# A new written order of the whole program, and engines chosen anew for its movable operations

## The chip, the cores and the metric

The kernel runs on one core of one Trainium2 chip. The metric is the device time of one execution in microseconds (us). The engines are named as in the profile: PE is TensorE (matmuls), PEld its weight loads, DVE is VectorE, ACT is ScalarE, POOL is GpSimd, SP is SyncE, whose queue issues the DMAs here.

## What is computed

Attention in both directions between 512 tokens x and 32 state tokens, for 8 batches and 8 heads of 64, and then a two-layer network with a squared ReLU on the 8 x 544 = 4352 rows that come out (512 wide, 2048 hidden). The weights w_in and w_out come as 64-bit floats.

```python
scores = scale * np.matmul(x, state.transpose(0, 1, 3, 2))
a = softmax(scores);  xread = np.matmul(a, state)
scores2 = scale * np.matmul(state, x.transpose(0, 1, 3, 2))
a2 = softmax(scores2);  sread = np.matmul(a2, x)
x = concatenate([xread, sread], axis=2) -> [4352, 512]
h = np.maximum(x @ w_in, 0.0)
out = h * h @ w_out
```

## The kernel before

Every matmul of the network keeps float32 accuracy with three passes: each operand is split into a high part (`*_hi`, rounded to fp32r by ACT) and a low part (`*_lo`, the rest, by a subtraction on DVE or POOL), and hi x hi, hi x lo and lo x hi are summed in PSUM. The rows xread are never formed: state @ w_in is made once for each batch (`direct_w2`, `second_w2`, later from a DRAM copy; tiles `w2ps`, `w2_<batch>_<hb>`), and the softmax, transposed (`k_hi`, `k_lo`), is multiplied with it.

The names that the change and the prediction touch:

- `warm.i` (line 855) is one dummy matmul of the identity into a tile `pw`. `prep.b.g` (631) transposes x through PE (`px`) and copies it out (`xT`); `states.0` does the same for the states (`pd`, `sD`), and `states.2` transposes those of the other batches on DVE (`sT<-std2`). `scores.b` writes `st`, `keep_s` copies it to `e2`, and `transposed_scores` transposes that to `pst`.
- `softmax.b.g` (717): a reduce to the maximum `m1` and a subtraction into `sp` on DVE, the exponential on ACT, a reduce, a small addition and a reciprocal on DVE, and a multiplication of `sp` (key `sm_mul`, POOL or DVE). Then PE transposes `sp` to `pa`, ACT rounds it to `k_hi`, and DVE subtracts to `k_lo`.
- `decode` (545) turns a 64-bit weight (`wi_raw`, `wo_raw`) into 32 bits (`wf`, `dec`): a clamp (keys `decode_wi`, `decode_wo`; DVE, or POOL where the key is listed), a Prelu on ACT, a shift on DVE, and an "or" with the low word on DVE (SCALAR_TENSOR_TENSOR). `prep_wo.fc` (1031) decodes w_out and splits it into `wo<fc>`: ACT makes the high part, and the key `w_out_lo` says whether POOL or DVE makes the low one.
- `hidden.blk.fc` (1039) makes one tile of 128 hidden units for 512 tokens in PSUM: six matmuls `ph<blk>_<fc>` from `k_hi`, `k_lo` and `w2`, then ReLU and square (ACT, or ACT and DVE), `g_hi` on ACT, and `g_lo = ph - g_hi` on DVE. The pool of `ph` has two buffers, so the tile after next can only begin when `g_lo` has been made. `accumulate.blk.fc` (1095) multiplies `g_hi`, `g_lo` with `wo<fc>` into four PSUM tiles `acc`. After every fourth hidden tile `acc` is copied to `first` or added to a partial sum.
- Batches 5 to 7 run later in a form with seven products in place of eight (`m`, `a_g`, `b_g`, `s`), and the 256 rows of sread come as a block 8.

Nothing is scheduled at run time or by a planner: `PLAN` (lines 25 to 340) is a list of 2835 step names written out. Each entry runs that step on to its next `yield`, and since `LOOSE_FROM` is "never", each engine's program is in exactly the order in which the entries are worked off. All instructions are issued through one helper, so the profile has them all at line 417, and tiles tell them apart. `SECOND` (368 to 404) lists the keys whose operation goes to the second of its two possible engines:

```python
def pick(key, *engs):
    return engs[chosen(key)]          # chosen: key in SECOND

def evac(key, out, src):
    if chosen(key): nc.vector.tensor_copy(out, src)
    else:           nc.scalar.copy(out, src)

for k in plan:
    if k not in begun:
        f, args, after = steps[k]
        begun[k] = f(*args)
    ...
        next(begun[k], None)
```

Of the kernel before, what the change touches and what calls it, by code (L numbers as in the profile page):

```python
# [30 lines left out]
        decode_wi.1 prep.1.0 transposed_scores.0.0 decode_wi.1 load_wo.1 direct_w2.0 softmax.0.1 direct_w2.0
        warm.12 softmax.0.1 direct_w2.0 softmax.0.1 warm.13 softmax.0.0 direct_w2.0 direct_w2.0 warm.14 softmax.0.0
        warm.15 direct_w2.0 softmax.0.0 warm.16 softmax.0.1 direct_w2.0 softmax.0.1 decode_wi.2 warm.17 second_w2.0
        softmax.0.0 softmax.0.0 prep_wo.1 prep_wo.0 prep_wo.0 warm.18 warm.19 second_w2.0 warm.20 second_w2.0
        warm.21 load_raw.3 prep.1.1 second_w2.0 second_w2.0 decode_wi.2 second_w2.0 prep.1.1 softmax.0.1 prep.1.1
        decode_wi.2 softmax.0.1 prep.1.0 load_wo.2 softmax.0.1 prep_wo.2 load_wo.8 decode_wi.2 prep.1.1 load_raw.4
        softmax.0.0 prep_wo.0 prep.1.0 load_wo.3 softmax.0.0 decode_wi.2 prep_wo.1 prep_wo.0 softmax.0.0 scores.1
        keep_s.1.0 decode_wi.3 load_states.2 keep_s.1.1 hidden.0.0 decode_wi.3 hidden.0.0 prep_wo.1 prep_wo.1
        hidden.0.0 decode_wi.3 prep_wo.0 hidden.0.0 transposed_scores.1.1 transposed_scores.1.0 decode_wi.4
        hidden.0.1 softmax.1.1 prep_wo.2 softmax.1.0 load_states.2 hidden.0.1 load_wo.4 softmax.1.1 prep_wo.3  # L40
        prep_wo.1 softmax.1.0 decode_wi.3 prep_wo.1 hidden.0.0 hidden.0.0 softmax.1.0 hidden.0.1 hidden.0.1
        accumulate.0.0 decode_wi.3 direct_w2.1 prep_wo.2 direct_w2.1 load_raw.5 accumulate.0.0 prep_wo.2
        direct_w2.1 direct_w2.1 direct_w2.1 decode_wi.4 direct_w2.1 direct_w2.1 softmax.1.1 hidden.0.1 load_wo.5
        second_w2.1 hidden.0.2 prep_wo.2 softmax.1.0 decode_wi.4 load_wo.7 hidden.0.1 accumulate.0.1 hidden.0.2
        hidden.0.2 decode_wi.4 softmax.1.0 load_raw.6 second_w2.1 second_w2.1 prep_wo.3 hidden.0.2 softmax.1.1
        hidden.0.3 softmax.1.0 accumulate.0.1 second_w2.1 decode_wi.4 prep_wo.2 hidden.0.3 softmax.1.0 exp_s.0.1
        hidden.0.2 hidden.0.2 softmax.1.1 second_w2.1 second_w2.1 load_wo.6 accumulate.0.2 hidden.0.3 exp_s.0.1
        prep_wo.3 softmax.1.1 decode_wi.5 decode_wi.5 prep_wo.3 softmax.1.1 softmax.1.0 hidden.0.3 load_states.2
        prep_wo.3 decode_wi.5 softmax.1.1 decode_wi.5 hidden.0.3 hidden.0.3 load_wo.11 decode_wi.5 prep_wo.4
        accumulate.0.2 hidden.1.0 decode_wi.6 prep_wo.3 direct_w2.2 load_raw.7 prep_wo.4 hidden.1.0 hidden.1.0  # L50
# [5 lines left out]
        decode_wi.7 accumulate.1.0 hidden.1.2 prep_wo.6 transposes.0 hidden.1.2 prep_wo.6 decode_wi.10 second_w2.2
        second_w2.2 prep_wo.6 hidden.1.2 prep_wo.5 second_w2.2 second_w2.2 second_w2.2 transposes.0 hidden.1.3
        hidden.1.2 hidden.1.2 decode_wi.10 hidden.1.3 accumulate.1.1 load_raw.8 prep_wo.4 decode_wi.10 direct_w2.3
        hidden.1.3 prep_wo.5 decode_wi.10 prep_wo.5 direct_w2.3 hidden.1.3 hidden.0.4 transposes.0 direct_w2.3
        direct_w2.3 accumulate.1.1 accumulate.1.2 load_wo.12 direct_w2.3 direct_w2.3 direct_w2.3 second_w2.3  # L60
        hidden.1.3 hidden.1.3 decode_wi.8 load_raw.11 hidden.0.4 transposes.0 second_w2.3 second_w2.3 hidden.0.4
        prep_wo.6 accumulate.1.2 decode_wi.8 second_w2.3 decode_wi.8 decode_wi.10 decode_wi.8 hidden.0.4 load_wo.13
        hidden.0.7 accumulate.1.3 prep_wo.5 prep_wo.6 prep_wo.4 hidden.0.7 accumulate.1.3 hidden.0.4 hidden.0.4
        prep_wo.9 hidden.0.7 decode_wi.11 hidden.0.7 load_raw.9 transposes.0 prep_wo.5 accumulate.1.3 decode_wi.11
        hidden.0.7 hidden.0.7 prep_wo.9 accumulate.1.3 accumulate.1.3 prep_wo.11 decode_wi.11 accumulate.1.3
# [1517 lines left out]
```

## Time and profile before

| | |
|---|---|
| median of 3 runs | 646.66 us (646.49 to 646.94) |
| the profiled execution | 646.96 us |
| its span in the trace | 645.1 us |
| PE busy | 631.9 us, 98% |
| PEld busy | 528.1 us, 82% |
| DVE busy | 465.8 us, 72% (927 instructions) |
| ACT busy | 394.7 us, 61% |
| POOL busy | 184.5 us, 29% (172 instructions) |

The span runs from the first to the last instruction on the engines; 1.9 us of the execution lie around it. A share of busy time is an average over stages that differ: in the first 80 us the weights are decoded and the softmaxes made while PE already multiplies; the middle part is multiplication with work for later batches beside it. In a timeline or a group, a row names the instruction as output<-inputs with buffer numbers left out, its shape, and in brackets the idle time of its engine just before it and what ended that. A stretch's row gives, behind its length, the busy time of PE, PEld, DVE, ACT and POOL, then TensorE's granted clock, the DMA engines' busy share and the GB/s.

### The profile page before, as it was taken

The page shows a single profiled execution, that of the slowest core. Times are in us where ns is not written, and L with a number is a line of the kernel's source. Part 1 is how long each engine was busy: PE and PEld are TensorE (multiplying, and loading weights), DVE is VectorE, ACT ScalarE, POOL GpSimd, SP SyncE. Part 2 cuts the span into 40 slices and gives each one's busy share as a digit, 9 for nine tenths or more (in the row PEclk, how much of TensorE's full clock was granted, in tenths as well). Part 3 has the DMA queues.
Part 4 walks back from the last instruction along what each step waited for, and adds up shares of the span by engine and source line. Part 5 has one row for each costly group of instructions (what it writes and reads, how often), then busy time and mean ns, then how long its engine had stood idle before and what let it go on. Part 6 is the DMA issues. An engine that isn't in the chain of part 4 may idle for free.

```text
span 645.1 us, 12288 instructions
## 1 busy us (share of the span) xinstructions
PE 631.9 (98%) x4453; PEld 528.1 (82%) x4453; DVE 465.8 (72%) x927; ACT 394.7 (61%) x815; POOL 184.5 (29%) x172
## 2 busy tenths in 40 slices
...
DVE  3999888675675688686958543579999866577637
...
GB/s 280 279 285 277 252 276 214 295 274 236 256 181 313 237 205 265 192 233 237 257 256 206 228 105 35 133 65 49 34 49 113 118 115 66 66 50 148 65 1 67
DMA packets 153132, 113.07 MB, mean 175 GB/s; under 512 B 93168, under 2 KB 126448, under 8 KB 153072
## 3 DMA queue, kind: packets, MB, share of 16 engines
...
q10 hardware_dynamic: 288, 0.26, 0.1%
...
## 4 chain that ended last, share of the span: by engine, by line
PE 94%; DVE 2%; issue 1%; DMA 1%; ACT 1%; SPq 0%; POOLq 0%; POOL 0%; DVEq 0%; ACTq 0%
PE acc L417 37%; PE ph L417 30%; PE m L417 18%; PE w2ps L417 3%; PE w4ps L417 2%; PE pr L417 1%; PE st L417 1%; PE pw L417 1%; DMA xn<-in_x_dram 1%; PE px L417 1%; DVE g_lo L417 1%; DVE ph L417 0%; PE pst L417 0%; ACT r L417 0%; PE pa L417 0%
## 5 line engine op out<-in xcount | busy, mean ns | idle before, releaser
L417 PE MATMUL acc<-wo,g_hi 128*128 128x512 f32 x704 | 203.8, 393 | 0.0
L417 PE MATMUL ph<-k_hi,w 128*128 128x512 f32 x512 | 176.1, 392 | 0.4 <-DVE g_lo L417 0.3
L417 PEld LDWEIGHTS acc<-wo,g_hi 128*128 128x128 f32 x704 | 130.6, 188 | 32.6 <-issue 2.5
L417 ACT ACTIVATE r<-ph 128x512 f32<-128x512 f32 (+1 forms) x124 | 70.4, 569 | 97.8 <-PE ph L417 92.6
L417 PE MATMUL acc<-wo,g_lo 128*128 128x512 f32 x352 | 122.1, 391 | 0.0
L417 PEld LDWEIGHTS ph<-k_hi,w 128*128 128x128 f32 x512 | 96.2, 188 | 21.4 <-issue 1.2
L417 PE MATMUL ph<-k_lo,w 128*128 128x512 f32 x256 | 100.3, 392 | 0.0
L417 PEld LDWEIGHTS acc<-wo,g_lo 128*128 128x128 f32 x352 | 65.7, 188 | 14.7 <-DVE dec L417 0.4
L417 DVE TENSOR_TENSOR g_lo<-ph,g_hi 128x512 fp32r<-128x512 f32 (+1 forms) x95 | 60.4, 640 | 23.3 <-ACT g_hi L417 18.9
L417 DVE SCALAR_TENSOR_TENSOR ph<-ph,r 128x512 f32<-128x512 f32 (+1 forms) x48 | 31.1, 648 | 42.3 <-ACT r L417 42.1
L417 PEld LDWEIGHTS ph<-k_lo,w 128*128 128x128 f32 x256 | 48.2, 188 | 8.2
L417 POOL TENSOR_TENSOR w<-w_f,w 128x512 fp32r<-128x512 f32 x21 | 28.9, 1383 | 74.1 <-ACT w L417 37.9
L417 POOL TENSOR_TENSOR sp<-sp,m 128x512 f32<-128x512 f32 x25 | 26.6, 1067 | 72.3 <-DVE m L417 67.5
L417 ACT ACTIVATE g_hi<-r 128x512 fp32r<-128x512 f32 (+1 forms) x76 | 44.0, 582 | 4.9 <-PE acc L417 3.8
L417 POOL TENSOR_TENSOR wf<-wf,wf_hi 128x512 fp32r<-128x512 f32 x8 | 10.9, 1367 | 67.9 <-ACT wf_hi L417 67.9
L417 ACT ACTIVATE ph<-ph 128x512 f32<-128x512 f32 x40 | 23.5, 587 | 10.1 <-PE ph L417 8.6
L417 ACT CAST w<-w_f 128x512 fp32r<-128x512 f32 x40 | 24.2, 614 | 6.6 <-DMA w_f<-w_d 6.5
L417 POOL TENSOR_SCALAR dec<-wo_raw 128x512 f32<-128x512 f32 x10 | 20.5, 2051 | 13.3 <-DMA wo_raw<-in_moe_w_out_dram 13.1
L417 ACT ACTIVATE g<-r 128x512 f32<-128x512 f32 x35 | 21.8, 630 | 0.4
L417 DVE TENSOR_REDUCE m<-sp 128x16 f32<-128x512 f32 x28 | 18.7, 670 | 3.3 <-ACT sp L417 3.1
L417 POOL TENSOR_TENSOR s<-sf,s 128x512 fp32r<-128x512 f32 x6 | 7.8, 1292 | 43.3 <-ACT s L417 43.3
L417 ACT COPY w4o<-w4ps 128x512 f32<-128x512 f32 x16 | 9.1, 588 | 13.8 <-PE w4ps L417 9.7
...
## 6 DMA issues: line engine op xcount, KB each, us to landing
...
```

Source lines behind the costliest of these rows:

```text
L417: op = call(*args, **kw)
```

## The change

`PLAN` is written anew from its 22nd entry on, to the end of the program: the same 2835 entries in another order. `SECOND` is chosen anew. PE, ACT and SP have as many instructions as before; DVE gets six more and POOL six fewer in sum, by many exchanges in both directions. The core of the diff (the table's other rows tell a reader nothing):

```diff
 PLAN = """
     ident warm.0 start.0 start.0 load.0.1 prep.0.0 warm.1 prep.0.0 warm.2 load_raw.0 load.0.1 load_states.0
-        prep.0.1 load_states.0 load_states.0 prep.0.1 warm.3 decode_wi.0 neg_ident load_raw.1 warm.4 prep.0.0
-        warm.5 start.1 warm.6 decode_wi.0 warm.7 prep.0.1 start.1 prep.0.0 load_wo.0 load.1.1 decode_wi.0
...
 SECOND = """
-    decode_wi: 4 10 11 12 13
-    decode_wo: 0 1 2 3 4 5 6 9 11 12
+    decode_wi: 4 11 12 14 15
+    decode_wo: 0 1 2 4 5 8 11 15
...
-    keep_s: 0.1
+    keep_s: 0.1 1.1
...
-    sm_mul: 3.0
+    sm_mul: 0.0 0.1 1.0 2.0 2.1 3.0 4.0 5.0 6.0 7.0 7.1
...
-    w_out_lo: 6 7 10 12 13 14 15
+    w_out_lo: 1 4 5 9 10 11 12 13
...
-    xT: 0.0.0 0.0.1 1.1.0
+    xT: 0.0.0 0.0.1 0.1.1
```

PE at the start of the program, before (px: transposes of x; pw: dummy matmuls; pd: transposes of the states; st: scores):

```order
L417 MATMUL px0_0_1_171<-ident_73,xn0_0_131 128x128 x4
L417 MATMUL pw5_176<-ident_73 128x128
L417 MATMUL pw6_182<-ident_73 128x128
L417 MATMUL pw7_185<-ident_73 128x128
L417 MATMUL px0_1_1_187<-ident_73,xn0_1_134 128x128 x4
L417 MATMUL pd_200<-ident_73,std0_150 128x128 x4
L417 MATMUL pw8_205<-ident_73 128x128
L417 MATMUL pw9_207<-ident_73 128x128
L417 MATMUL st0_1_215<-xT0_1_152,sD_122 32x256
```

and with the change:

```order
L420 MATMUL px0_0_1_176<-ident_73,xn0_0_131 128x128 x4
L420 MATMUL px0_1_1_181<-ident_73,xn0_1_134 128x128 x4
L420 MATMUL pd_190<-ident_73,std0_150 128x128 x4
L420 MATMUL pw6_203<-ident_73 128x128
L420 MATMUL pw21_205<-ident_73 128x128
L420 MATMUL st0_1_214<-xT0_1_152,sD_122 32x256
```

The transposes of x and of the states follow each other, and the first scores come after two dummy matmuls instead of five.

DVE in the first softmaxes, before (m10, sp0: softmax of batch 0; wf, dec: decodes of weights):

```order
L417 TENSOR_SCALAR wf1_315<-wi_raw2_211 128x512
L417 TENSOR_REDUCE m10_0_297<-sp0_0_296 128x16
L417 TENSOR_SCALAR m10_0_297<-m10_0_297 128x16
L417 RECIPROCAL m10_0_297<-m10_0_297 128x16
L417 TENSOR_SCALAR dec0_254<-dec0_254 128x512
L417 COPY xT1_1_341<-px1_1_0_342 128x512
L417 TENSOR_SCALAR wf1_315<-wf1_315 128x512
L417 TENSOR_TENSOR k_lo0_130<-pa0_1_352,k_hi0_129 128x512
L417 SCALAR_TENSOR_TENSOR wf1_315<-wi_raw2_211,wf1_315 128x512
L417 SCALAR_TENSOR_TENSOR dec0_254<-wo_raw0_194,dec0_254 128x512
L417 TENSOR_TENSOR k_lo0_130<-pa0_0_380,k_hi0_129 128x512
```

and with the change:

```order
L420 RECIPROCAL m10_1_289<-m10_1_289 128x16
L420 TENSOR_TENSOR sp0_1_288<-sp0_1_288,m10_1_289 128x512
L420 TENSOR_SCALAR wf1_333<-wi_raw2_201 128x512
L420 TENSOR_SCALAR dec0_258<-dec0_258 128x512
L420 TENSOR_REDUCE m10_0_293<-sp0_0_292 128x16
L420 TENSOR_SCALAR m10_0_293<-m10_0_293 128x16
L420 RECIPROCAL m10_0_293<-m10_0_293 128x16
L420 TENSOR_TENSOR sp0_0_292<-sp0_0_292,m10_0_293 128x512
L420 TENSOR_SCALAR wf1_333<-wf1_333 128x512
L420 SCALAR_TENSOR_TENSOR wf1_333<-wi_raw2_201,wf1_333 128x512
L420 TENSOR_TENSOR k_lo0_130<-pa0_1_352,k_hi0_129 128x512
L420 TENSOR_TENSOR k_lo0_130<-pa0_0_377,k_hi0_129 128x512
```

Both multiplications of sp0 now stand on DVE. The copy of xT1_1 and the or of dec0 no longer stand ahead of the last k_lo0.

DVE ahead of the hidden tiles 4 to 7 of block 0, before (g_lo0_7 is the row that the tile ph0_5 waits for):

```order
L417 TENSOR_SCALAR wf4_860<-wi_raw8_801 128x512
L417 TENSOR_TENSOR w2_1_3_857<-w2ps3_0_0_806,w2_1_3_857 128x256
L417 TENSOR_SCALAR wf4_860<-wf4_860 128x512
L417 SCALAR_TENSOR_TENSOR wf4_860<-wi_raw8_801,wf4_860 128x512
L417 TENSOR_TENSOR wo6_870<-dec6_716,wo6_870 128x512
L417 TENSOR_TENSOR g_lo0_4_865<-ph0_4_831,g_hi0_4_864 128x512
L417 SCALAR_TENSOR_TENSOR ph0_7_884<-ph0_7_884,r0_7_905 128x512
L417 TENSOR_TENSOR g_lo0_7_904<-ph0_7_884,g_hi0_7_903 128x512
```

and with the change:

```order
L420 TENSOR_TENSOR w2_0_3_847<-w2ps3_0_1_830,w2_0_3_847 128x256
L420 TENSOR_TENSOR w2_1_3_864<-w2ps3_0_0_829,w2_1_3_864 128x256
L420 STREAM_TRANSPOSE sT_121<-std2_531 128x768
L420 TENSOR_SCALAR wf4_861<-wf4_861 128x512
L420 SCALAR_TENSOR_TENSOR wf4_861<-wi_raw8_810,wf4_861 128x512
L420 TENSOR_TENSOR wo5_871<-dec5_655,wo5_871 128x512
L420 SCALAR_TENSOR_TENSOR ph0_7_882<-ph0_7_882,r0_7_891 128x512
L420 TENSOR_TENSOR g_lo0_4_849<-ph0_4_822,g_hi0_4_848 128x512
L420 TENSOR_TENSOR w2_1_3_864<-w2ps3_0_1_830,w2_1_3_864 128x256
L420 TENSOR_SCALAR wf5_787<-wf5_787 128x512
L420 SCALAR_TENSOR_TENSOR wf5_787<-wi_raw11_814,wf5_787 128x512
L420 TENSOR_TENSOR g_lo0_7_890<-ph0_7_882,g_hi0_7_889 128x512
```

Between w2_0_3 and g_lo0_7 there are now the transpose sT, wo5 in the place of wo6, one w2 more, and the second half of wf5.

## Rows read from the trace of the kernel before

**Rows 1.** Page: DVE in 40 slices (tenths); chain that ended last, by engine.

```profile
DVE  3999888675675688686958543579999866577637
...
PE 94%; DVE 2%; issue 1%; DMA 1%; ACT 1%; SPq 0%; POOLq 0%; POOL 0%; DVEq 0%; ACTq 0%
```

**Rows 2.** Waits of PE, whole span: released by, us in total, times, longest.

```profile
PE ph L417 <- DVE g_lo L417: 1.2, 3, 0.6
PE w4ps L417 <- DVE g_lo L417: 1.0, 1, 1.0
PE w2ps L417 <- DVE wf L417: 0.6, 1, 0.6
```

**Rows 3.** Stretches of the span: length, then busy us (instructions) of each engine.

```profile
16.10:32.30 16.20, 15.38 (x154) 11.13 (x160) 15.67 (x29) 13.84 (x30) 11.05 (x7) 1.00 0.88 278
32.30:48.40 16.10, 16.06 (x128) 11.96 (x109) 15.64 (x32) 14.08 (x31) 11.15 (x9) 1.00 0.88 285
```

**Rows 4.** Timeline of PE, 0 to 17 us: start, duration, engine, operation, tiles.

```profile
9.49 1.49 PE L417 MATMUL pw<-ident 128*128 128x128 f32 x6
10.77 1.06 PE L417 MATMUL px<-ident,xn 128*128 128x128 f32 x4
...
13.23 1.09 PE L417 MATMUL st<-xT,sD 64*32 64x256 f32 x32
```

**Rows 5.** Timeline of DVE, 14 to 26 us.

```profile
15.02 0.42 DVE L417 TENSOR_SCALAR wf<-wf 128x512 uint32<-128x512 uint32 x1
15.47 0.69 DVE L417 SCALAR_TENSOR_TENSOR wf<-wi_raw,wf 128x512 uint32<-128x512 uint32 x1
16.08 0.68 DVE L417 TENSOR_REDUCE m<-pst 128x16 f32<-128x512 f32 x1
...
24.62 0.68 DVE L417 TENSOR_TENSOR k_lo<-pa,k_hi 128x512 fp32r<-128x512 f32 x1
```

**Rows 6.** Groups on DVE, 24.6 to 67 us: count, busy us, mean ns, idle before.

```profile
L417 DVE SCALAR_TENSOR_TENSOR dec<-wo_raw,dec 128x512 uint32<-128x512 uint32 x7 | 6.8, 975 | 0.1
L417 DVE SCALAR_TENSOR_TENSOR wf<-wi_raw,wf 128x512 uint32<-128x512 uint32 x7 | 6.1, 871 | 0.1
L417 DVE TENSOR_TENSOR w<-w2ps,w 128x256 fp32r<-128x256 f32 x11 | 4.3, 409 | 0.0
L417 DVE TENSOR_SCALAR wf<-wf 128x512 uint32<-128x512 uint32 x7 | 3.8, 546 | 1.3 <-ACT wf L417 1.3
L417 DVE TENSOR_SCALAR wf<-wi_raw 128x512 f32<-128x512 f32 x5 | 3.0, 603 | 0.0
L417 DVE TENSOR_SCALAR dec<-dec 128x512 uint32<-128x512 uint32 x6 | 3.0, 499 | 0.0
```

**Rows 7.** Groups on POOL, 24.6 to 67 us.

```profile
L417 POOL TENSOR_SCALAR dec<-wo_raw 128x512 f32<-128x512 f32 x8 | 16.5, 2071 | 0.5 <-DMA wo_raw<-in_moe_w_out_dram 0.4
L417 POOL TENSOR_TENSOR wo<-dec,wo 128x512 fp32r<-128x512 f32 x6 | 8.9, 1490 | 3.9 <-ACT wo L417 3.9
L417 POOL TENSOR_SCALAR wf<-wi_raw 128x512 f32<-128x512 f32 x3 | 5.8, 1947 | 5.3 <-DMA wi_raw<-in_moe_w_in_dram 5.3
L417 POOL TENSOR_TENSOR sp<-sp,m 128x512 f32<-128x512 f32 x2 | 2.1, 1051 | 2.9 <-DVE m L417 2.9
```

**Rows 8.** Waits of DVE, 24.6 to 67 us.

```profile
DVE wf L417 <- ACT wf L417: 1.3, 2, 1.0
```

**Rows 9.** Timeline of DVE, 66 to 92 us.

```profile
66.92 0.69 DVE L417 TENSOR_TENSOR g_lo<-ph,g_hi 128x512 fp32r<-128x512 f32 x1
...
91.32 0.96 DVE L417 STREAM_TRANSPOSE sT<-std 128x768 f32<-128x768 f32 x1
```

**Rows 10.** Timeline of PE: at 68 us, and at 195.8 us.

```profile
67.98 0.39 PE L417 MATMUL ph<-k_hi,w 128*128 128x512 f32 x1
68.21 0.39 PE L417 MATMUL ph<-k_lo,w 128*128 128x512 f32 x1
...
195.77 0.38 PE L417 MATMUL w4ps<-wf_hi,s 64*128 64x256 f32 x1 [1.05 <-DVE g_lo L417]
```

More of the change, by code (lines that the diff above doesn't have):

```diff
@@ L31 @@
[L31 to L50, printed above, removed]
@@ L56 @@
[L56 to L65, printed above, removed]
@@ new lines @@
+        load_w2.2.1 accumulate.1.11 load_w2.2.0 later_w2.3 later_w2.3 later_w2.3 later_w2.3 later_w2.3 later_w2.3
+        start.3 start.3 prep.2.1 later_w2.3 load_w2.2.0 hidden.1.14 hidden.1.14 hidden.1.14 hidden.1.14
+        scores.2+read.1 transposed_scores.2.0 load_w2.2.2 load_w2.3.0 split_wf.4 load_wf.1.5 softmax.2.0
+        softmax.2.0 softmax.2.0 hidden.1.14 hidden.1.14 transposed_scores.2.1 softmax.2.1 softmax.2.1 softmax.2.0
+        softmax.2.1 load_w2.2.1 softmax.2.0 softmax.2.0 exp_s.2.1 softmax.2.0 softmax.2.0 accumulate.1.12
@@ new lines @@
+        hidden.2.7 hidden.2.7 hidden.2.7 hidden.2.7 later_w2.7 later_w2.7 read.2 sread.2 load.4.1 load.4.1 sread.2
+        sread.2 sread.2 load_w2.2.6 hidden.2.8 hidden.2.8 hidden.2.8 hidden.2.8 accumulate.2.7 load_w2.2.5
+        load_w2.2.5 hidden.2.8 hidden.2.8 w2.1+scores.3 transposed_scores.3.0 last_w2.1 last_w2.1 load_wf.2.0
+        load_wf.2.2 exp_s.3.0 last_w2.1 accumulate.2.8 last_w2.1 load_w2.2.7 last_w2.1 last_w2.1 start.5
+        softmax.3.0 transposed_scores.3.1 softmax.3.1 start.5 start.5 prep.4.0 softmax.3.1 exp_s.3.0 exp_s.3.1
@@ new lines @@
+        start.5 load.5.1 load_w2.2.6 load_w2.2.6 hidden.2.11 hidden.2.11 hidden.2.11 hidden.2.11 hidden.2.11
+        hidden.2.11 hidden.2.10 hidden.2.10 accumulate.2.9 exp_s.3.0 hidden.2.10 hidden.2.10 hidden.2.10
+        hidden.2.10 hidden.2.12 exp_s.3.1 load_w2.2.7 hidden.2.12 accumulate.2.10 exp_s.3.1 transposes.3 load.5.1
+        load.5.1 load.5.1 prep.4.1 load_w2.3.0 transposes.3 hidden.2.12 hidden.2.12 hidden.2.12 hidden.2.12
+        softmax.3.0 softmax.3.0 softmax.3.0 softmax.3.0 softmax.3.1 w2.0+scores.4 last_w2.0 softmax.3.0 softmax.3.0
@@ new lines @@
+        hidden.3.1 load_w2.3.3 load_w2.3.2 start.6 load_w2.3.3 hidden.3.3 hidden.3.3 hidden.3.3 hidden.3.2
+        accumulate.2.15 accumulate.2.15 hidden.3.2 hidden.3.3 hidden.3.3 load_w2.3.4 softmax.4.0 softmax.4.0
+        load_w2.3.5 load.6.1 load_w2.3.6 accumulate.3.0 accumulate.3.1 softmax.4.0 read.3 hidden.3.2 hidden.3.2
+        transposes.4 softmax.4.0 transposes.4 hidden.3.2 hidden.3.2 softmax.4.0 load.6.1 softmax.4.0 softmax.4.1
+        softmax.4.1 sread.3 sread.3 sread.3 w2.2+scores.5 softmax.4.1 last_w2.2 last_w2.2 transposed_scores.5.0
```

617 lines of the change are left out of this document (316 added, 301 removed).

## Prediction, made before the changed kernel was run

> **What bounds the kernel now.** I read the page first, then what TensorE (PE) waits for, then the busy time by stretch, then the rows of the engines that feed PE. Of the chain that ended last 94% is PE's [rows 1]. So no order of the same instructions can gain more than the little PE time that is idle, and every us that PE waits longer is lost for good, since nothing behind it has slack to give it back. That idle time is small and named: 1.2 us at three of ph and 1.0 at one of w4ps, all behind a g_lo on VectorE (DVE), 0.6 at one of w2ps behind a wf on DVE [rows 2], and a start in which PE waits for data.
>
> The stretches show which engine comes next. From 16.1 us on, while the weights are decoded and PE already multiplies, DVE is busy 15.67 of 16.20 us and then 15.64 of 16.10 [rows 3]. There DVE, not PE, is nearly full; GpSimd (POOL) is busy 11 of 16. PE gets through because DVE finishes each piece just before it is wanted. This is where a new order and a new choice of engines weigh most. The slices of the page show one more such place: DVE stands at 9 in slices 28 to 31, from some 435 to 500 us [rows 1].
>
> **The change, term 1: the start.** In the old order three dummy matmuls pw5 to pw7 stand between two transposes of x. Their row begins at 9.49 us and the next transpose at 10.77 [rows 4]: 1.28 us, which the new order puts off until after the scores' inputs. So st0 (13.23 us before) can start up to 1.28 us earlier, if the copies that feed it keep up: the copy of px0_1_1 goes to DVE and leaves ACT free. Behind st0 stand, on DVE, the copy of e, a shift, the or of a decode and the first softmax reduce at 16.08 [rows 5], in the same order as now; all shift together. But both softmax multiplications of batch 0 leave POOL (1051 ns each, [rows 7]) for DVE and now stand in its queue before k_lo0_0, which gates the first hidden matmuls. One of the two lies beside work that DVE had to wait through anyway (the exponential on ACT); the other adds a place of 0.60 (a 512-column row starts 0.60 to 0.61 after the one before: 15.47 to 16.08). I take 1.28 - 0.60 = **0.7 us earlier** for k_lo0_0 (24.62 before, [rows 5]). The ends are 0 (both multiplications in series) and 1.28.
>
> **Term 2: DVE between k_lo0_0 and g_lo0_7.** ph0_5 starts at 67.98 us in the trace [rows 10], right behind g_lo0_7 (66.92 to 67.61, [rows 9]): ph has two buffers, and g_lo0_7 is the last reader of the one that ph0_5 writes. I count DVE's instructions from k_lo0_0 to g_lo0_7 in both orders. The new order has fifteen more and one fewer:
> - seven of 512 columns at 0.60: the copy of e2 of batch 1 (from ACT), the or of dec0 (from ahead of k_lo0_0), the or of the second half of wf5, the low halves of wo1, wo4 and wo5 (from POOL), and the multiplication of sp1_0 (from POOL): 4.2 us;
> - four clamps or shifts (dec3, dec6, twice wf5), whose row is 0.42 and which give way 0.08 before their end: 4 x 0.34 = 1.4;
> - a reduce of m21 with its small scaling, about 0.7 (a reduce is 0.68 long, [rows 5]), put forward;
> - the transpose of the states sT, 0.96 long at 91.32 in the trace [rows 9], put forward by some 25 us: 0.9;
> - one low half of w2 (409 ns, [rows 6]): 0.3;
> - the low half of wo6 goes to POOL: -0.6.
>
> Sum: **+6.9 us**. Next, the order inside: where an instruction reads what the one right ahead of it wrote, the next start is 0.45 after a shift of 0.42 (15.02 to 15.47, [rows 5]) and not 0.34, that is 0.11 more. The old order has 15 such neighbours in this stretch, the new one 26: 11 x 0.11 = **+1.2 us**.
>
> Against this stands relief. Shifts, clamps and ors of the decode run longer here than undisturbed: dec or 975 ns against 690 at 15.47 in seven, wf or 871 in seven, wf shift 546 against 420 in seven, wf clamp 603 in five, dec shift 499 in six [rows 5, 6]. That is 7 x 0.285 + 7 x 0.18 + 7 x 0.126 + 5 x 0.18 + 6 x 0.08 = 5.5 us in all. The long ones lie beside POOL instructions, and POOL's work in the stretch falls: eight clamps dec, six wo, three wf and two sp, 16.5 + 8.9 + 5.8 + 2.1 = 33.3 us [rows 7], become three dec, two wf, three wo and one sp, 6.2 + 3.9 + 4.5 + 1.1 = 15.7. I scale the lengthening with POOL's busy time, so 53% of 5.5 goes: **-2.9 us**. Last, DVE idled 1.3 us there waiting for ACT [rows 8]. I leave that as it is: the new order also has DVE wait, for matmuls that are themselves late. Ends: -1.3 and 0.
>
> g_lo0_7 then starts at 66.92 - 0.7 + 6.9 + 1.2 - 2.9 = **71.4**, and ph0_5 at 71.4 + 0.69 + 0.06 = 72.2 (the step from a late g_lo to its matmul is 0.06 by what follows). PE has the same matmuls ahead of ph0_5 as now, except that the six of ph0_6 come before it and not after: six pitches of 0.23 (67.98 to 68.21, [rows 10]), 1.4 us. Unchanged, it would stand at 67.98 + 1.4 = 69.4. So PE is **2.8 us later** here. The wait does not fall on ph0_5 alone: k_lo1, the copies of first and w2_0_3 are queued behind the same DVE rows and are late by smaller amounts before it. They are part of the 2.8, not added to it. Behind g_lo0_7, the clamps of dec9 and dec7 and the copy of first1_1 come; they were late already and set nothing more.
>
> **Term 3: later waits.** At 195.77 PE waits 1.05 us for g_lo2_5 [rows 10], because on DVE it stands behind several copies of w4o; the new order puts it directly behind g_lo2_2. I count 0.6 of it as gained; the ends are 0 and 1.0. A delay that PE already has does not help or hurt later, since DVE is shifted with it. In the stretch from 435 us on, where DVE is full again, about as many low halves and sums go from POOL to DVE as come the other way, so I cost it at nothing; the cover is that DVE keeps up, and PE's waits for g_lo on ph, 1.2 us in three [rows 2], give the ends: -0.8 if those go, +1.2 if as much again is added. Other copies change between ACT and DVE where neither is full, and cost nothing.
>
> **Sum:** 2.8 - 0.6 = +2.2 us. The profiled execution is 646.96 us (span 645.1 and 1.9 around it), which gives 649.2. It lies 0.3 above the median 646.66, so the median to expect is **648.9 us**.
>
> **One rule that would turn this.** POOL and DVE run beside each other for most of the stretch: 33.3 us of POOL work [rows 7] lengthened DVE's by 5.5 only. The Trainium skill, page Perfetto Trace Analysis, section Optimizing Scalar/DVE Operations, says that the two share an SBUF read port, so that moving operations between them might not help. By it, POOL's old instructions had held DVE up for about as long as they lasted, and the moved ones would cost DVE nothing net. The sum would then come out near rival A, below. The trace agrees only in part, with 5.5 of 33.3 us.
>
> **Rivals.**
> - **A, faster: the lengthening goes altogether.** If nearly all 5.5 us of lengthening and the 1.3 of idle time are used up, g_lo0_7 starts at 74.3 - 6.8 = 67.5 (74.3 is 71.4 without the relief). PE meets ph0_5 unhindered at 69.4 - 0.7 = 68.7, for which g_lo0_7 has to start by 67.9. So this decides from 6.4 us of relief on, of the 6.8 that there is. Then only gains are left: 0.7 at the start, 0.6 at w2ps, 0.6 at 195 us: 646.7 - 1.9 = 644.8. For it speaks that the worst rows lie beside POOL; against it that POOL keeps 15.7 us of work, and that the moved low halves and multiplications, which read two tiles in SBUF, may be lengthened in their turn.
> - **B, no change.** Relief of about 5 us leaves ph0_5 late by 0.7 us, and the gain at 195 pays for it: 646.7 + 0.7 - 0.6 = 646.8. It needs the other waits of the stretch to stay hidden.
> - **C, slower by more: no relief.** The moved instructions meet POOL's remaining ones as often as before, g_lo0_7 starts at 74.3, PE is 5.7 us late: 646.7 + 5.7 - 0.6 = 651.8.
>
> That the change does not do what it says is no rival: each engine's program follows the written order.
>
> **How the numbers follow.** A measurement of this kernel can tell about 0.2%, 1.3 us, from no change. The forecast gets 0.58 (0.46 of it above +1.3 us, 0.12 below, since less idle or a quicker start takes 1 us off easily); A 0.17; B 0.15; C 0.10. Faster 0.17, same 0.27, slower 0.56. The range runs from 645.2 (A with three quarters of its gains) to 652.2 (C with little gained at 195 us): what lies outside is the better part of A, and C with a start that gains nothing or new waits from 435 us on. The forecast's own range is 647.0 to 651.0.
>
> **What would show it.** Right: k_lo0_0 before 24.3 us; DVE without gaps from 25 to 70 us, with POOL near half its work; new waits of PE behind g_lo, k_lo, first or w2 between 33 and 72 us; ph0_5 at about 72; the wait at 195 us smaller. Wrong: DVE's ors and shifts all at 0.42 and 0.69 us and ph0_5 before 69 us (A), or PE waits of over a us in the fast blocks, where I counted nothing.

## The result and the profile after

The changed kernel took 653.39 us (median of 4 runs, 652.72 to 654.58) against 646.8 for the kernel before on the same chip (4 runs, 646.49 to 647.44): a ratio of 1.0103, 95% interval 1.0085 to 1.012. It is slower by 6.6 us. The forecast was 648.9 with a range to 652.2: the direction was right, the size was not. The profiled execution took 652.72 us with a span of 650.9, 5.8 more than the span before; the accounts below are made against these 5.8. (In the trace of the change PE was 0.95 us ahead before the two programs differ, told of below; without that lead the 5.8 would be 6.8.)

Two lines of its page answer to [rows 1]: DVE in 40 slices, and the chain that ended last.

```profile
DVE  4998899764786579788867534679999784667547
...
PE 83%; DVE 10%; ACT 3%; issue 2%; DMA 1%; SPq 0%; POOL 0%; POOLq 0%; DVEq 0%; ACTq 0%
```

PE's share of the chain fell from 94% to 83%, DVE's rose from 2 to 10. Where, the chain of 20 to 76 us tells. Before, its parts by line:

```profile
by line: PE acc L417 44.3%; PE ph L417 29.0%; PE w2ps L417 7.4%; PE px L417 3.1%; PE pa L417 3.1%; PE st L417 2.6%; issue 2.4%; DVE m L417 2.3%; PE pst L417 2.0%; PE pw L417 1.8%; DVE sp L417 1.3%; DVE wf L417 1.3%; DVEq L417 0.0%
```

After, pieces of the same chain in order of time (start, us, what):

```profile
32.69 0.69 DVE dec L420
33.38 0.60 DVE wo L420
33.98 0.34 DVE w L420
34.32 0.60 DVE m L420
...
34.95 1.10 DVE m L420
...
36.36 0.69 DVE sp L420
37.05 0.35 DVE w L420
...
37.69 0.64 ACT sp L420
...
38.35 0.70 DVE m L420
```

Summed over its pieces, the chain from 20 to 76 us lay on PE for 52.3 us before and on DVE for 2.8; after, it lies on DVE for 35.6, on ACT for 10.3 and on PE for 7.1. PE no longer bounds these 56 us; DVE does for most of them, and there a row put ahead of those that PE needs can delay PE. The waits of PE, over the whole span, answer to [rows 2]:

```profile
PE ph L420 <- DVE g_lo L420: 2.3, 3, 1.3
PE w2ps L420 <- DVE wf L420: 1.6, 2, 1.4
PE ph L420 <- ACT w4o L420: 0.7, 1, 0.7
PE ph L420 <- DVE k_lo L420: 0.5, 1, 0.5
PE w4ps L420 <- DVE g_lo L420: 0.2, 1, 0.2
```

The wait of w4ps at 195 us is gone but for 0.2 (1.05 in [rows 10]). In its place PE waits at six rows between 30 and 74 us; three of them, in PE's timeline:

```profile
30.88 1.69 PE L420 MATMUL w2ps<-wf,sD 64*32 64x256 f32 x32 [1.40 <-DVE wf L420]
...
46.40 0.50 PE L420 MATMUL ph<-k_lo,w 128*128 128x512 f32 x1 [0.53 <-DVE k_lo L420]
...
73.84 0.50 PE L420 MATMUL ph<-k_hi,w 128*128 128x512 f32 x1 [1.31 <-DVE g_lo L420]
```

The last is ph0_5, forecast at 72.2 us. Before, the w2ps of the first row waited less:

```profile
31.92 1.10 PE L417 MATMUL w2ps<-wf,sD 64*32 64x256 f32 x32 [0.63 <-DVE wf L417]
```

The stretches answer to [rows 3]:

```profile
16.10:32.30 16.20, 14.56 (x140) 11.02 (x139) 15.86 (x30) 13.43 (x28) 7.54 (x4) 1.00 0.70 258
32.30:48.40 16.10, 14.75 (x75) 10.61 (x63) 15.46 (x32) 10.89 (x23) 5.74 (x4) 1.00 0.73 219
```

DVE is as full as before, POOL has 7.54 and 5.74 us of work for 11.05 and 11.15, and now PE and ACT stand still instead (ACT 10.89 for 14.08). The groups of DVE from 23 to 73 us answer to [rows 6]:

```profile
L420 DVE SCALAR_TENSOR_TENSOR wf<-wi_raw,wf 128x512 uint32<-128x512 uint32 x8 | 7.2, 902 | 0.3
L420 DVE SCALAR_TENSOR_TENSOR dec<-wo_raw,dec 128x512 uint32<-128x512 uint32 x7 | 5.8, 826 | 0.2
...
L420 DVE TENSOR_SCALAR wf<-wf 128x512 uint32<-128x512 uint32 x8 | 3.3, 409 | 0.8 <-ACT wf L420 0.7
L420 DVE TENSOR_SCALAR wf<-wi_raw 128x512 f32<-128x512 f32 x6 | 3.0, 504 | 0.0
...
L420 DVE TENSOR_SCALAR dec<-dec 128x512 uint32<-128x512 uint32 x6 | 2.5, 415 | 0.0
...
L420 DVE TENSOR_SCALAR m<-m 128x16 f32<-128x16 f32 x2 | 1.3, 630 | 0.1
```

The shifts are undisturbed now (409 and 415 ns); the ors are not (902 and 826 against 690), and the small scaling m, some 0.17 long elsewhere, has a mean of 630. Four rows make nearly all of that. On DVE:

```profile
25.43 1.66 DVE L420 SCALAR_TENSOR_TENSOR dec<-wo_raw,dec 128x512 uint32<-128x512 uint32 x1
...
34.95 1.09 DVE L420 TENSOR_SCALAR m<-m 128x16 f32<-128x16 f32 x1
...
39.91 1.40 DVE L420 SCALAR_TENSOR_TENSOR wf<-wi_raw,wf 128x512 uint32<-128x512 uint32 x1
...
71.52 1.67 DVE L420 SCALAR_TENSOR_TENSOR wf<-wi_raw,wf 128x512 uint32<-128x512 uint32 x1
73.11 0.68 DVE L420 TENSOR_TENSOR g_lo<-ph,g_hi 128x512 fp32r<-128x512 f32 x1
```

And on POOL:

```profile
25.27 1.28 POOL L420 TENSOR_TENSOR wo<-dec,wo 128x512 fp32r<-128x512 f32 x1 [5.76 <-ACT wo L420]
...
34.71 1.30 POOL L420 TENSOR_TENSOR wo<-dec,wo 128x512 fp32r<-128x512 f32 x1 [3.90 <-ACT wo L420]
39.71 1.05 POOL L420 TENSOR_TENSOR sp<-sp,m 128x512 f32<-128x512 f32 x1 [3.70 <-DVE m L420]
...
71.07 1.56 POOL L420 TENSOR_TENSOR wo<-dec,wo 128x512 fp32r<-128x512 f32 x1 [2.23 <-ACT wo L420]
```

Each long row of DVE begins 0.16 to 0.45 us after a two-input row of POOL, and the three ors end 0.54 to 0.56 after that row's end (27.09 and 26.55; 41.31 and 40.76; 73.19 and 72.63), that is, after nearly an or's own length; the scaling ends with it (36.04 and 36.01). So DVE stood still until POOL's row was through: about 1 us each in three, 0.7 in one. The kernel before has such stops too, five of 0.5 to 1.1. The Trainium skill, page SBUF — State Buffer, section Who interferes with whom, calls the pair of ports that the two share an exclusive lock: a DVE instruction with two SBUF inputs and a POOL instruction that reads SBUF, or a DVE instruction in a 2-port mode and any of POOL's, block each other fully, the one that came first going first. The three ors, which read two tiles, agree; the scaling reads one, and no row shows in which mode it ran.

Behind POOL's clamps, which read one tile, the trace agrees only in part. An or on DVE, and the clamp on POOL inside which it lies:

```profile
30.04 0.69 DVE L420 SCALAR_TENSOR_TENSOR wf<-wi_raw,wf 128x512 uint32<-128x512 uint32 x1
```

```profile
28.87 1.94 POOL L420 TENSOR_SCALAR wf<-wi_raw 128x512 f32<-128x512 f32 x1
```

This or is not longer at all. Counted over the traces of all 16 kernels of this document, from 14 to 110 us: of 36 ors that begin inside a two-input row of POOL 31 are 0.5 to 1.1 us longer than 0.69; of 110 that begin inside a clamp only 27 are, by 0.2 to 0.5, those that begin in its first part; of 243 that meet no row of POOL, none.

In the changed kernel these stops stand right ahead of what PE needs: that of dec1 at 25.43 ahead of the or of wf1, for which w2ps waits 1.40 at 30.88; that of wf5 at 71.52 ahead of g_lo0_7, for which ph0_5 waits 1.31; that of m at 34.95 ahead of a low half of w2_0_1, for which ACT's whole queue stands still:

```profile
37.42 0.37 ACT L420 CAST w<-w2ps 128x256 fp32r<-128x256 f32 x1 [2.58 <-DVE w L420]
37.69 0.64 ACT L420 ACTIVATE sp<-sp 128x512 f32<-128x512 f32 x1
```

Behind that cast on ACT are the exponential of sp1_1 and the ReLU of ph0_2.

### The profile page after: what moved, and what is told of

Read it like the earlier page. It is cut to its first block, busy times and chain, and to the rows that moved or that the text cites. A ratio compares the mean times of both kernels' runs of the same rounds, so it can differ in the third digit from the quotient of the medians.

```text
span 650.9 us, 12302 instructions
## 1 busy us (share of the span) xinstructions
PE 634.8 (98%) x4453; PEld 526.6 (81%) x4453; DVE 476.6 (73%) x933; ACT 394.0 (61%) x815; POOL 175.1 (27%) x166
## 4 chain that ended last, share of the span: by engine, by line
PE 83%; DVE 10%; ACT 3%; issue 2%; DMA 1%; SPq 0%; POOL 0%; POOLq 0%; DVEq 0%; ACTq 0%
PE acc L420 32%; PE ph L420 27%; PE m L420 17%; PE w2ps L420 2%; DVE m L420 2%; PE w4ps L420 2%; DVE wf L420 2%; DVE sp L420 1%; PE pr L420 1%; PE st L420 1%; DVE g_lo L420 1%; DVE dec L420 1%; ACT ph L420 1%; DVE k_lo L420 1%; DMA xn<-in_x_dram 1%
## 5 line engine op out<-in xcount | busy, mean ns | idle before, releaser
L420 POOL TENSOR_TENSOR sp<-sp,m 128x512 f32<-128x512 f32 x11 | 12.2, 1111 | 55.4 <-DVE m L420 39.2
L420 POOL TENSOR_TENSOR wf<-wf,wf_hi 128x512 fp32r<-128x512 f32 x12 | 16.5, 1384 | 34.3 <-ACT wf_hi L420 24.3
L420 ACT ACTIVATE g<-r 128x512 f32<-128x512 f32 x39 | 23.8, 630 | 0.4
L420 POOL TENSOR_SCALAR dec<-wo_raw 128x512 f32<-128x512 f32 x8 | 16.9, 2116 | 19.0 <-DMA wo_raw<-in_moe_w_out_dram 19.0
L420 POOL TENSOR_TENSOR s<-sf,s 128x512 fp32r<-128x512 f32 x7 | 9.4, 1355 | 43.5 <-ACT s L420 30.9
L420 DVE COPY w4o<-w4ps 128x512 f32<-128x512 f32 x18 | 11.9, 682 | 9.6 <-PE w4ps L420 5.0
```

The lines of the kernel that those rows point to most:

```text
L420: op = call(*args, **kw)
```

## The experiments

Fourteen kernels were run against the kernel before. Besides the time, one number is followed: PE's **lag**, the start of a matmul minus its start in the trace of before, taken only where both have issued the same matmuls up to there. In us; each column is one matmul, named by its start before, and the last is the difference of the spans. e6, e8 and e11 have the start of the kernel before, and yet lags of -1.41, 1.07 and -0.31 at the first column: so much does one execution's start differ from the next. Lags are therefore compared from each kernel's own start.

| kernel | 25.69 | 31.92 | 43.69 | 65.26 | 80.11 | 102.20 | 178.04 | 314.18 | 444.27 | end |
|---|---|---|---|---|---|---|---|---|---|---|
| the change | -1.44 | -1.04 | 1.09 | 2.85 | 4.66 | 4.98 | 5.10 | 5.20 | 5.25 | 5.81 |
| e1 | -0.07 | -0.81 | 1.09 | 3.62 | 5.96 | 9.02 | 13.77 | 16.81 | 19.22 | 21.04 |
| e2 | 1.09 | 1.22 | 0.94 | 1.16 | 1.16 | 1.16 | 2.47 | 5.68 | 6.63 | 8.63 |
| e3 | -0.64 | 2.31 | 1.97 | 1.97 | 1.97 | 1.97 | 1.97 | 2.00 | 2.26 | 2.22 |
| e4 | -0.74 | 0.66 | 0.29 | 0.32 | 0.32 | 2.36 | 2.51 | 2.68 | 2.74 | 3.32 |
| e5 | -0.19 | 0.20 | 2.32 | 4.08 | 6.34 | 6.61 | 6.77 | 6.85 | 6.89 | 7.45 |
| e6 | -1.41 | -1.95 | -2.11 | -2.14 | -2.14 | -2.14 | -2.13 | -2.13 | -1.86 | -1.90 |
| e7 | -0.51 | -0.10 | 2.04 | 3.26 | 3.93 | 6.02 | 6.18 | 6.31 | 6.35 | 6.86 |
| e8 | 1.07 | 0.85 | 0.86 | 0.86 | 0.86 | 0.86 | 0.86 | 0.73 | 0.45 | 0.77 |
| e9 | -1.94 | -1.54 | 0.28 | 1.62 | 3.42 | 3.75 | 3.90 | 4.09 | 4.14 | 4.71 |
| e10 | -1.78 | -2.86 | -0.88 | 0.95 | 4.12 | 5.98 | 6.13 | 6.25 | 6.31 | 6.87 |
| e11 | -0.31 | -0.89 | -0.95 | -0.95 | -0.95 | -0.95 | -0.95 | -0.68 | -0.43 | -0.39 |
| e12 | -0.74 | -1.82 | 0.19 | 1.98 | 2.25 | 4.17 | 4.33 | 4.46 | 4.46 | 5.04 |
| e13 | -0.76 | -0.96 | 0.26 | 3.21 | 4.08 | 6.14 | 6.29 | 6.44 | 6.46 | 7.28 |
| e14 | -0.49 | -1.54 | 0.29 | 2.97 | 3.23 | 5.31 | 5.46 | 5.57 | 5.58 | 6.48 |

In the diffs below the entries of `PLAN` stand one on a line; an entry repeated is the step's next piece.

**e1 and e2: the order and the engines apart.** e1 is the new order with the old engines, e2 the old order with the new.

The diff is that of e1 against the change:

```diff
 SECOND = """
-    decode_wi: 4 11 12 14 15
+    decode_wi: 4 10 11 12 13
-    decode_wo: 0 1 2 4 5 8 11 15
+    decode_wo: 0 1 2 3 4 5 6 9 11 12
...
```

> The new order with the old choice of engines. Theory 1 (the choice of engines filled DVE: of the +6.9 us of DVE work ahead of g_lo0_7 about 3.5 us are instructions taken over from POOL): about 3 us of the 6.6 us loss go, so near 650. Theory 2 (the order alone lost the time: urgent rows stand behind decode work on DVE whoever runs the rest): no better than the change, 653 or more, since POOL is slower at the same instructions. Theory 3 (POOL's presence lengthens DVE): DVE's ors and shifts get longer again, and the time is worse than the change.

> The old order with the new choice of engines. Theory 1: most of the loss is here too, 650 or more, with PE waiting for DVE between 30 and 75 us. Theory 2: within 1 us of the kernel before. Either way its first 7 us are the same program as the kernel before, so its second wait of PE for xn shows whether the 0.95 us by which that transpose came earlier in the changed kernel is chance.

e1 took 667.57 us (ratio 1.0326, 1.0298 to 1.0354), e2 655.4 (1.0144, 1.0117 to 1.017). The order alone is far worse than both together, the engines alone by 2 us, where the two intervals overlap. In e2 PE loses 1.1 by 25.7 us, at the first k_lo, and then nothing up to 102, although DVE has eight more rows than before between k_lo0_0 and g_lo0_7 (84 for 76: nine more, four of them clamps, and one fewer). At the prediction's steps of 0.60 and 0.34 that is 3.8 us; the interval is 43.13 us long for 42.31, 0.8 more. DVE's long rows are shorter there by some 1.7 us in sum, and its idle time is 1.5 us for 2.3. So most of what the moved rows cost came back there. That is near what the prediction drew from the Trainium skill, page Perfetto Trace Analysis, section Optimizing Scalar/DVE Operations, that such moves might not help because the two engines share an SBUF read port. What costs up to 102 us is the order: e1, which has it without the engines, loses 9.1 by then. Behind 125 us it is the other way about: e2 loses 7.5 more, the change 1.0.

**e3 and e4: the order by stages.** e3 has the new order up to the first matmuls of ph0_0, then the old; e4 the new start, the old order to the hidden tile 0.9 (some 95 us), then the new, each with the engines of the part in hand.

```diff
 warm.4
-prep.0.0
-warm.5
...
```

> New order and engines up to the first matmul of ph0_0, old ones after it. The aligned traces put PE 1.4 us ahead at that point. If the start is worth that and nothing behind it takes it back: 645.3 or so. If the new start only leaves DVE with work it put off (the or of dec0, the copy of e21) that is missing later: 646 to 648.

> As e3 up to about 95 us (old order and engines from ph0_0 to the first step of hidden tile 9), and the new ones after that. By the aligned traces the change loses 6.1 us between 25 and 75 us and 1.2 us in all behind 100 us: about 646.5. If the loss sits elsewhere, or moves to where old and new meet, 650 or more.

e3 took 649.24 us (1.005, 1.0033 to 1.0067), e4 651.4 (1.0084, 1.0061 to 1.0107). With the old order from 26 us on, the lag falls slightly from 32 to 80 us (2.31 to 1.97; 0.66 to 0.32), where the change loses 5.7: the loss belongs to the new order of this stretch. In e4 the seam costs 2.0 between 80 and 102 and the later stages, as the new order has them, 1.0 more. Both pay at the first seam, where eight matmuls acc wait equally long. PE's timeline of e3, and its stretch behind that wait:

```profile
30.67 3.63 PE L410 MATMUL acc<-wo,g_hi 128*128 128x512 f32 x8 [2.19 <-ACT g_hi L410]
```

```profile
30.60:34.40 3.80, 3.73 (x16) 2.68 (x24) 3.77 (x6) 3.17 (x7) 2.63 (x2) 0.55 0.54 164
```

The same two views of e4:

```profile
30.56 2.09 PE L410 MATMUL acc<-wo,g_hi 128*128 128x512 f32 x8 [2.19 <-ACT g_hi L410]
```

```profile
30.60:34.40 3.80, 3.80 (x43) 2.54 (x44) 3.77 (x7) 3.68 (x9) 2.53 (x2) 1.00 0.52 174
```

After the same wait the granted clock was 0.55 in one and 1.00 in the other: near the lower of the two levels, 1.2 GHz, against the full 2.4. The eight matmuls took 3.63 us for 2.09; that is most of the 1.65 by which the two lags differ at 31.9 us.

**e5 to e8: moving single rows.** e5 is the change with sT, the reduce of m21 and the last shift and or of wf5 put back behind g_lo0_7; e6 is the kernel before with sT and m21 put forward. From the diff of e6:

```diff
 hidden.1.3
+states.2
 decode_wi.8
...
 load_w2.0.4
-states.2
 hidden.1.7
```

> The changed kernel, with four pieces of DVE work that it had put forward set back behind g_lo0_7: the transpose sT (and its rounding on ACT), the reduce m21 with its scaling, and shift and or of the second half of wf5, 2.6 us of DVE together. If DVE's queue ahead of g_lo0_7 is what PE waits for (my term 2): g_lo0_7 about 2.5 us earlier and 651 us. If the chain of urgent rows and their waits sets the pace, and not the length of the queue: g_lo0_7 less than 1 us earlier, 652.5 or more.

> The kernel before, with only the transpose sT and the reduce m21 put forward to where the change has them, 1.65 us of DVE work ahead of g_lo0_7. Queue theory: ph0_5 is late by up to 1.6 us, 647 to 648.3. If DVE's idle time of 1.9 us in that stretch takes them in: within 0.4 us of the kernel before.

e5: 654.55 us (1.0132, 1.0112 to 1.0152). DVE's interval is 2.45 shorter and PE gains 1.8 behind ph0_5, counted from each kernel's start; but at 86.45 it waits 1.84 for a copy w2o on DVE and has lost it. e6: 646.34 (1.0006, 0.9989 to 1.0024): the same rows put forward cost the old order nothing, since its chain from 20 to 76 us stays on PE (55.9 of 56 us). The price of a row depends on which engine heads the chain.

e7 is the change with nine pairs of a shift and its or drawn apart by a row; e8 the kernel before with two steps moved, so that its waits at 195 and 444 us go. From the diff of e7:

```diff
 decode_wi.7
-decode_wi.7
 second_w2.2
 second_w2.2
+decode_wi.7
```

> The changed kernel, with nine of the shift-and-or pairs of the decode no longer next to each other on DVE (each or one place later; the or of wf5 behind g_lo0_7). My estimate of 0.11 us for a pair: 1.0 us, and 0.6 for the or of wf5: g_lo0_7 1.5 us earlier, 652. If the pairs cost nothing where DVE waits anyway: 653.

> The kernel before with two entries moved: the second half of w4ps5 on PE behind the matmuls of hidden tile 2 (so that g_lo2_5 is there when its buffer is wanted: the wait of 1.05 us at 195.77), and one low half of w2 on DVE behind g_lo8_13 (the wait of 0.61 at 444.27). If both waits are only a matter of order: 1.6 us faster, 645. If the waits come back at the next use of the buffers: no change.

e7: 653.62 us (1.0117, 1.0098 to 1.0136): the interval is 2.35 shorter (47.58), PE gains 2.0 behind ph0_5 and loses it by 102 (0.45 at a wo on POOL, 0.70 at a g_lo). e8: 646.04 (1.0002, 0.9981 to 1.0022): both named waits went, and the lag gained 0.3 and 0.8 there and lost as much in small waits before and behind. No better.

**e9 to e12: the rows that PE waits for first.** e9 is the change with both low halves of w2_0_1 ahead of the reduce and scaling of sp1_0; e11 the kernel before with the change's order around that cast. The diff of e9:

```diff
 direct_w2.1
+direct_w2.1
+direct_w2.1
 softmax.1.0
 softmax.1.0
-direct_w2.1
-direct_w2.1
```

> The changed kernel, with one DVE row moved: the second low half of w2_0_1 goes ahead of the reduce, the reciprocal and the multiplication of sp1_0. Theory 4 (ACT's queue stood still behind DVE's): ACT's idle 2.58 us at its cast of w2_1_1 all but goes, the exponential of sp1_1 starts by 35.5 us and not at 37.7, and PE gains 1.5 to 2.5 us by 46 us: 651 to 652. Theory 1 (length of DVE's queue alone): DVE has the same work, so no gain behind 46 us: 653.4.

> The kernel before, with only the order around that cast as in the change: on DVE the low half of w2_0_1 behind the reduce of sp1_0, on ACT the casts of w2_1_1 ahead of the exponential of sp1_1. No work added, no engine changed. Theory 4: ACT stands still some 2 us, the exponential comes 2.5 us or more later, PE waits before ph1_0: 648 or more. Theory 1: no change, 646.2.

e9: 652.85 us (1.0099, 1.0082 to 1.0116). ACT's stop of 2.58 is gone, and the lag grows by 2.2 from 25.7 to 43.7 us and not by 2.5. The gain may be larger than that: in this execution the granted clock, which stood at 1.00 there in the change, fell behind a wait of 1.41 at 30.38. Two stretches of e9:

```profile
32.00:34.00 2.00, 2.00 (x11) 1.62 (x6) 1.97 (x5) 2.00 (x6) 0.00 (x0) 0.54 0.74 260
34.00:36.00 2.00, 2.00 (x7) 1.53 (x7) 1.90 (x5) 2.00 (x6) 1.28 (x1) 0.61 1.02 312
```

DVE's interval up to g_lo0_7 is 0.73 shorter (49.20). e11: 646.73 (1.0002, 0.9988 to 1.0017): in the old order the same arrangement makes ACT wait 0.94 and costs PE nothing. The stop of ACT was thus a sign of DVE being late, and a cause of its own of about 0.7 us, as far as one trace with a lowered clock can tell.

e10 joins e5, e7 and e9 and puts the shift and or of dec1 behind the or of wf1; e12 is e10 with DVE's two copies w2o ahead of the shifts and ors of dec7 and dec9. From the diff of e12 against e10:

```diff
 direct_w2.4
+direct_w2.4
+direct_w2.4
+direct_w2.5
+direct_w2.5
+direct_w2.5
+prep_wo.7
 prep_wo.9
...
```

> The changed kernel with the move of e9, shift and or of dec1 behind those of wf1, and the moves of e5 and e7 together; engines as in the change. If what the change lost between 25 and 75 us is its order of rows on DVE and ACT: 4 us or more come back, 649 or less. If it is the choice of engines: 651 or more.

> The kernel of the last experiment but one (urgent rows first: 652.96 against 646.4 before), with one more exchange around 80 us: DVE's two copies of w2ps into w2o stand ahead of the shifts and ors of dec7 and dec9, for whose Prelu on ACT DVE stood still for 1.71 us, and not behind them. If the loss there is this one wait (1.83 us of TensorE at 84.23 and the 1.8 us that it lost at a granted clock of 0.56 to 0.59), the lag at 102 us falls from 5.95 to 2.5 or less, the clock stays above 0.9 from 84 to 88 us, and the time is 649 to 650.5. If DVE is late as a whole there, the next row waits in its place (the ors of dec7 and dec9, then wo7, wo9 or g_lo1_4), the lag at 102 us stays above 4, and the time stays within 1 us of 653.

e10: 652.96 us (1.0097, 1.008 to 1.0115). ph0_5 comes at 70.30 without a wait, and at 65 us the lag is 2.7 above the start's where the change's is 4.3. Then one wait takes it all back; its row in PE's timeline, and the two stretches there:

```profile
84.23 0.69 PE L410 MATMUL ph<-k_hi,w 128*128 128x512 f32 x1 [1.83 <-DVE w2o L410]
```

```profile
84.00:86.00 2.00, 1.77 (x4) 1.39 (x5) 1.89 (x3) 0.94 (x3) 2.00 (x2) 0.59 0.76 253
86.00:88.00 2.00, 2.00 (x7) 1.56 (x6) 1.60 (x2) 1.20 (x3) 2.00 (x2) 0.56 1.01 293
```

The granted clock falls to 0.59 and 0.56 for four us, and nine matmuls start 0.43 us after each other instead of 0.23: 1.8 us more on top of the wait. In e12 that wait is gone, and in the stretches of 2 us from 80 to 90 the clock stays at 1.00. Yet PE waits 0.47 for a wo on POOL and 0.46 for a g_lo, the lag at 102 us is 4.17, and the time is 652.1 (1.0102, 1.0083 to 1.0121). The next late row had taken the place of the one mended, as the second theory said.

**e13 and e14: POOL's two-input rows taken away.** e13 is the change with the five two-input rows of POOL between 24 and 75 us on DVE (four low halves of wo, one multiplication of sp); e14 does much the same to e12. From the diff of e13 against the change:

```diff
-    w_out_lo: 1 4 5 9 10 11 12 13
+    w_out_lo: 0 1 2 3 4 5 6 9 10 11 12 13
...
-    sm_mul: 0.0 0.1 1.0 2.0 2.1 3.0 4.0 5.0 6.0 7.0 7.1
+    sm_mul: 0.0 0.1 1.0 1.1 2.0 2.1 3.0 4.0 5.0 6.0 7.0 7.1
```

> The changed kernel, with five of GpSimd's two-input rows between 24 and 75 us put on DVE (the low halves of wo0, wo2, wo3, wo6 and the multiplication of sp1_1); the low half of wo0 stands right behind a clamp, the others where their steps stand. In the changed kernel four of these five began just before a DVE row, and that row ended 0.54 to 0.56 us after GpSimd's: the or of dec1 1.66 long at 25.43, the scaling of m11_0 1.09 at 34.95, the or of wf2 1.40 at 39.91, the or of wf5 1.67 at 71.52, together 3.6 us over their usual length. Theory that these stops hold up the rows TensorE waits for: none of the four is over its usual length by 0.3, ACT's stop of 2.58 at 37 us falls to some 1.7, TensorE's wait on wf at 31 us falls from 1.40 to 0.4 to 1.0, its wait at ph0_5 from 1.31 to 0.3 or less, and its lag at 75 us falls from 4.65 to about 3 (3.6 less of stops, 2.4 more of rows ahead of g_lo0_7). Rival, that only the number of DVE's rows and their order count: with five more rows of 0.6 the lag at 75 us is 4.6 to 7, and the waits stay.

> The kernel with the urgent rows and the two copies w2o first (652.1 against 645.7 before), with five of GpSimd's two-input rows put on DVE too (the low halves of wo2, wo3, wo6, wo7 and the multiplication of sp1_1). There the stops between 24 and 90 us are 0.71 at m11_0, 0.71 at wf2 and 0.43 at wf6. If stops behind GpSimd's two-input rows are what is left, the lag at 102 us falls from 4.14 to about 3 and the time is 650.5 to 651.5; if DVE's number of rows is, it rises to 4.5 to 6 and the time is 652.5 to 654.

e13: 653.14 us (1.0113, 1.0092 to 1.0135). The four stops are gone, and the interval up to g_lo0_7 is 1.28 us shorter with four more rows in it (48.65, 94 rows). On DVE, the row that was 1.67 long, and the g_lo behind it:

```profile
71.91 0.70 DVE L410 SCALAR_TENSOR_TENSOR wf<-wi_raw,wf 128x512 uint32<-128x512 uint32 x1
72.52 0.69 DVE L410 TENSOR_TENSOR g_lo<-ph,g_hi 128x512 fp32r<-128x512 f32 x1
```

The waits that hung on them shrink, as the theory of the stops had it: 1.40 to 0.80 and 1.31 to 0.32 on PE (the rows below), 2.58 to 1.67 on ACT.

```profile
30.96 1.69 PE L410 MATMUL w2ps<-wf,sD 64*32 64x256 f32 x32 [0.80 <-DVE wf L410]
...
73.26 0.50 PE L410 MATMUL ph<-k_hi,w 128*128 128x512 f32 x1 [0.32 <-DVE g_lo L410]
```

But the wait for k_lo grows from 0.53 to 0.78 (45.82), a new one of 0.41 comes at 47.20 (a low half of wo, now on DVE), the lag at 80 us is 4.08 for 4.66, nearer to the rival's 4.6 than to the 3 that the theory gave (from each kernel's own start, 4.8 for 6.1), and by 102 it is 6.14. In e14 the lag at 102 us rises from 4.17 to 5.31, and the time is 653.45 (1.0119, 1.0094 to 1.0144), as the rival had forecast; but what makes it is again one row: PE waits 1.67 at 89.02 for the low half of wo7, one of the rows moved to DVE, where it had waited 0.47 for it on POOL. So taking the stops away changes on which row PE waits; it does not lessen what PE has lost by 102 us.

## Why the prediction was wrong in size

**Term 1, the start: met, but not shown to be the change's doing.** k_lo0_0 starts at 23.18 us (24.62 before; forecast 23.9, and before 24.3). Of PE's lead of 1.44 at 25.7 us, 0.95 is there already at the first transposes that wait for x's second piece, where both programs are still alike: how soon that DMA lands differs from run to run. That leaves 0.5; the forecast was 0.7. But the same subtraction gives -0.2 to 0.8 in the ten traces that have the new start and engines, and 1.0, -0.6 and -0.5 in e6, e8 and e11, which start the old way. So the 0.5 is no larger than what one start differs from the next, and nearly two thirds of the lead were luck.

**Term 2, DVE up to g_lo0_7: the step that failed.** The place, the gate and the count of rows held: 90 rows for 76, and g_lo0_7 is what ph0_5 waits for. But the interval grew from 42.31 to 49.93 us, 7.6, where the terms gave 6.9 + 1.2 - 2.9 = 5.2. The failing term is the relief of **-2.9**, with the idle time that was to stay. The kinds that made 5.5 us of lengthening [rows 5, 6] still make 8 x 0.212 + 7 x 0.136 + 6 x 0.084 = 3.15, and the scaling of m adds 0.9 that was not there: 1.4 us of relief for 2.9. The scaling by POOL's busy time was the mistake. A stop comes where a DVE row meets a POOL row already begun, and the long ones come from POOL's two-input rows (wo, sp), of which there are five from 24 to 75 us where there were eight; most of the work that left POOL was clamps [rows 7], whose stops were the shorter ones. And DVE's waits for ACT in the interval are 2.8 us (1.3 for a g_hi, 0.8 for a wf, 0.5 for an e, 0.2 for others) against 1.8 (the 1.3 of [rows 8], 0.3 for an r and 0.2 for a k_hi). They do not come from ACT's stop behind DVE at 37 us: e9, which has no such stop, has the same three (1.28, 0.80 and 0.56). The rows of ACT show where the longest comes from:

```profile
47.16 0.73 ACT L420 ACTIVATE e<-e,m 128x512 f32<-128x512 f32 x1 [1.02 <-DVE m L420]
...
47.88 1.19 ACT L420 ACTIVATE ph<-ph 128x512 f32<-128x512 f32 x2
```

The new order has this exponential of e ahead of the ReLU and square of ph1_0, and the old one had it behind them; the matmuls of ph1_0 are through at 47.13, and the g_hi that DVE waits for comes behind both. For the other two the cause stays open. The two terms make 1.5 + 1.0 = 2.5 us where 2.4 were missing; the count of rows and pairs was 0.1 too high. So PE is 4.65 late behind ph0_5 and not 2.8.

**The lead at the start** was counted as kept up to g_lo0_7. PE had spent part of it by 32 us: the wait for wf1 is 1.40, and the 32 matmuls behind it take 1.69 us instead of the 1.10 in the kernel before, at a granted clock of 1.00; no row says why (they take 1.69 in e13 too and 1.09 in e14, behind waits of 0.80 and 1.09 us).

**Term 3: right, but not alone.** The wait at 195 us falls from 1.05 to 0.20, and the lag there by 0.94 (0.6 forecast, ends 0 and 1.0). But just before, at 193.92, ph2_2 waits 0.67 for a copy w4o on ACT, which I had costed at nothing, and with smaller waits the lag at 314 us is 0.1 above that at 178. Of the rest costed at nothing, 80 to 178 us cost 0.4 and the stretch behind 314 us 0.6. From 80 us to the end that is +1.15 where the forecast had -0.6.

The account of the spans: 4.65 + 1.15 = 5.8, for 2.8 - 0.6 = 2.2. Of the 3.6 missing, 1.85 belong to term 2 and 1.75 to what was costed at nothing or paid back.

**The rivals.** A (all relief, faster) and B fell: DVE was late by more, not by less. C came nearest, 651.8, but its cause, no relief at all, is not what the rows show: there was relief of 1.4, and more idle time. That PE's waits would fall on g_lo, k_lo and w2 was right; those behind ACT and at w2ps were not on the list, because I followed DVE's queue and PE's, and not ACT's, which stands between them.

**What stays open.** Every version of the whole new order run here loses 5 to 9 us of PE's time by 102 us, measured from its own start at 25.7, whichever waits are mended. Which of the rows that the order puts forward are worth that, the runs do not tell one by one; e5, e7 and e13 show that two or three at a time do not give it back. Loads may be part of it: between 20 and 76 us the chains of e5, e9 and e10 lie on loads for 6.0, 4.3 and 12.3 us, that of the change on none, and in e10 a load of 7.12 us on it begins right behind an or on DVE (67.15). No run takes the two apart. No version run here beats the kernel before: e6, e8 and e11 equal it.
